# Moments ahead of a set-up chain, and PSUM banks handed out in adjacent pairs

## The chip, the cores and the metric

One core of one Trainium2 chip. The metric is the device time of one execution in microseconds (us), the median of the runs. The profile comes from one execution under the hardware profiler.

## The reference

Two layers, A and B, are applied in turn, twice, each on the layer norm of x and added to x (x is 2048 x 512, fp32).

```python
def _A_ref(x, w_r, w_i):
    X = rfft2(x); X = X * (w_r + 1j * w_i)
    return irfft2(X, s=(S, D))

def _B_ref(u, ...):
    K = einsum("dn,dnl,dn->dl", Cc, exp(dt*A*l), dt*Bc).real      # 512 x 2048 kernel of a state space
    y = irfft(rfft(u padded) * rfft(K padded))[:L]                # causal convolution, column by column
    return y + u * Dskip

x = x + _A_ref(_layernorm(x), ...)
x = x + _B_ref(_layernorm(x), ...)
x = x + _A_ref(_layernorm(x), ...)
x = x + _B_ref(_layernorm(x), ...)
```

## The kernel before

x lies in SBUF as 16 rows of [128, 512]. The Fourier transforms are matmuls with tables. The program is cut into pieces, Python generators that yield what their next step needs: an engine, a free tile of a ring, PSUM banks ("p:" and a kind), or an event such as `self.after(("in", 0))`. A planner, class Clock, holds a rough cost for each instruction and walks all pieces of a phase: among the steps that could start first by its own clock it emits the one with the smallest rank, the number given beside the piece. The order in which it emits is the order in each engine's queue; the hardware runs every queue in that order.

The first phase holds layer A of round 0 and the building of B's kernel K:

- `loads` sends the 8 pairs of x's rows on SP's queue, and between them the tables and, by `load_n`, the arrays kN (`ld` and two parts of `an`) from which K is made.
- `moments` (L494, L495) takes mean and variance of a row on DVE. `spread` (L502, L504, L507) makes the factors of four rows' norm, with a square root on ACT.
- `forward_a` normalises a row on ACT (L517), adds and subtracts its halves on POOL (L544 to L549), multiplies on PE (L562 to L571) and copies to SBUF on ACT (L576). `first_a` then needs all 16 rows: it folds (L589), multiplies by the weights (L687 to L704) and goes back (L713 to L725).
- The set-up, `setup_b` (rank -130; L1071 to L1117) and `setup_a` (-110; L1034 to L1049), is a chain of small DVE and ACT steps on kN. `setup_f` and `parts` split its results into three bf16 parts each by casts on ACT (L1020) and subtractions on DVE (L1026), which go to DRAM (`spe`, `spt`). When all 15 are there, `load_k` (L1126, L1127) brings back slices of them, and `exp_k` (L1135, L1151) and `unit_k` (L1165 to L1195) make K in 32 units.

Then ranks from -4 on mix the units with `first_a` and the inverse `inv_a`. In the second phase come B of round 0, A of round 1 (`forward_a` with r = 1, `group_a`, `inv_a`) and B of round 1. `group_b` makes a spectrum by matmuls into two banks X (L829), multiplies it by the kernel's on DVE (L929), combines on POOL (L935), and goes back on PE (L946) and ACT (L955); `group_a` does the like for A: L626, then L631 to L633 on DVE, L637 on POOL, L646 and L649 on PE. `forward_b` turns rows of x (L796, L798), `inv_b` adds B's result to x (L973, L979).

PSUM has 8 banks of 512 columns, shared out by kind:

```python
BANKS1, SAME1 = {'a': (0, 2, 4), 's': (6, 7)}, {'t': 's', 'h': 's', 'l': 's', 'x': 's', 'k': 'a'}
BANKS2 = {'x': (0, 1, 2, 3), 't': (4, 5), 'h': (6, 7)}
```

In the second phase a piece that wants two banks for its products asks for "p:x p:x" and gets any two of the four.

Of the kernel before, what the change touches and what calls it, by code (L numbers as in the profile page):

```python
# [11 lines left out]
OP = mybir.AluOpType  # L12
# [7 lines left out]
BANKS1, SAME1 = {'a': (0, 2, 4), 's': (6, 7)}, {'t': 's', 'h': 's', 'l': 's', 'x': 's', 'k': 'a'}  # L20
BANKS2 = {'x': (0, 1, 2, 3), 't': (4, 5), 'h': (6, 7)}

# [383 lines left out]
class Net:  # L406
# [28 lines left out]
    def psum(self, kind):  # L435
        kind = self.same.get(kind, kind)

        banks = self.banks[kind]

        def make(i):  # L440
            o = 512 * banks[i]
            return self.ps[:, o:o + (1024 if kind == "a" else 512)]
        return self.timer.tile("p:" + kind, make, len(banks))
# [26 lines left out]
    def loads(self):  # L470

        src = self.io["A_x"].rearrange("b (p s) d -> p (b s) d", p=128)
        for q in range(8):
            self.nc.sync.dma_start(self.x[:, 2 * q:2 * q + 2, :], src[:, 2 * q:2 * q + 2, :])
            self.mark("in", q)
            yield self.emitted(("in", q))
            for i, f in ((0, "load_ra"), (1, "load_n"), (5, "load_da"), (6, "load_h"), (7, "load_rb")):
                if i == q:
                    getattr(self, f)()
            if q == 1:  # L480
                self.mark("kN")
                yield self.emitted("kN")
# [51 lines left out]
    def forward_a(self, r, s2, st):  # L534
# [16 lines left out]
        if r:  # L551
# [5 lines left out]
            self.drop(uv)  # L557
        yield "PE p:x"
        p = self.psum("x")
        R, R2, nR = self.Ra[:, 1], self.Ra.rearrange("p a m -> p (a m)"), self.Ra[:, 2]  # L560
# [31 lines left out]
    def group_a(self, g):  # L592
# [29 lines left out]
        self.drop(AB)  # L622
        yield "PE p:x p:x"
        X = [self.psum("x")[:, :257] for sg in range(2)]
        for sg in range(2):
            nc.tensor.matmul(X[sg], ca[:, sg, :], V[:, sg, :257], start=True, stop=True)  # L626
        self.drop(V)
        yield "DVE t1a t2a"
        t1, t2 = (self.w(k, [128, 2, 258]) for k in ("t1a", "t2a"))
        for sg in range(2):  # L630
            nc.vector.tensor_tensor(t1[:, sg, :257], X[sg], W[:, 0, sg], op=OP.mult)  # L631
            nc.vector.scalar_tensor_tensor(t2[re, sg, :257], X[sg][im], -1.0, W[im, 1, sg], op0=OP.mult, op1=OP.mult)
            nc.vector.tensor_tensor(t2[im, sg, :257], X[sg][re], W[re, 1, sg], op=OP.mult)  # L633
        self.drop(*X)
        yield "POOL Za"
# [27 lines left out]
    def first_a(self, r, g):  # L663
# [16 lines left out]
        if r:  # L680
            nc.gpsimd.memset(Y2[:, 64:65], 0.0)
        yield "PE p:x p:x" if r else "PE p:a"
        X = [self.psum("x") for _ in range(2)] if r else [self.psum("a")]
        Xr, Xi = X if r else (X[0][:, :512], X[0][:, 512:])
        P, Q, nP = ca[:, 0, :], ca[:, 1, :], ca[:, 2, :]
# [12 lines left out]
        nc.vector.tensor_tensor(t2[:, 1, :], Xi[:, :257], W[:, 0, :257], op=OP.mult)  # L698
        self.drop(*X)
        yield "POOL Za"  # L700
# [99 lines left out]
    def forward_b(self, r, b, e, st):  # L800


        free = self.emitted(("group", 1), 16) if r else self.emitted(("inverse", 0), 16) if e else self.after("product", 32)
        yield "DVE a", self.after((id(st), b // 2) if not r else (id(st), b // 2, b % 2)), free
        xn = self.w("a", [128, 2, 256])
        for s in range(2):
            self.norm(2 * b + s, st, slice(256 * e, 256 * e + 256), xn[:, s])
        one = not (r or e)
        yield "PE p:a yd" if one else "PE p:x p:x iy"
        y = self.w("yd" if one else "iy", [128, 2, 512])  # L810
        self.turn_b([xn[:, 0], xn[:, 1]], y, "a" if one else "xx")
# [75 lines left out]
    def group_b(self, r, q, e):  # L887
# [16 lines left out]
        if new:  # L904
            y = self.w("yk", [128, 2, 2, 256])
            nc.sync.dma_start(y.rearrange("p g h d -> p g (h d)"), self.yk[1, two].rearrange("g c a b h d -> (c a b) g (h d)"))
            yield "PE p:x p:x", self.emitted("gk", q + 1)
            gk = self.gk[q]
            K = [self.psum("x") for _ in range(2)]
            self.spectrum(gk, [y[:, j] for j in range(2)], K)  # L910
            self.drop(gk, y)
            yield "ACT"
            for j in range(2):
                nc.scalar.copy(kh[:, j].rearrange("p r d -> p (r d)"), K[j])
            nc.scalar.dma_start(self.khat[:, two, :, d], kh)
            self.drop(*K)
            yield "+"
        Y = self.place[e][:, two].rearrange("p g (h d) -> p g h d", h=2)
        yield "PE p:x p:x", self.after(("rows", r, e), 8), self.after(("gi", r, q)), self.emitted(("added", r), 16)
        gi = self.gi[r, q]  # L920
        X = [self.psum("x") for _ in range(2)]
        self.spectrum(gi, [Y[:, j] for j in range(2)], X)
        names = ("t1b", "t2b", "Zb") if r else ("t1", "t2", "Z")
        yield f"DVE {names[0]} {names[1]}"
        t = [self.w(k, [128, 2, 2, 256]) for k in names[:2]]
        for j in range(2):
            for c in range(2):
                x = X[j].rearrange("p (r d) -> p r d", r=2)[:, c, None, :].to_broadcast([128, 2, 256])
                nc.vector.tensor_tensor(t[c][:, j], x, kh[:, j, ::-1, :] if c else kh[:, j], op=OP.mult)  # L929
        self.drop(*X, kh)  # L930

# [26 lines left out]
    def inv_b(self, r, b, e, st=None):  # L958
# [8 lines left out]
        late = not e and b > 4  # L967
        yield "PE p:x p:x" if late else "PE p:h p:t", self.emitted(("turned", r), 8 * late)
        q = [self.psum(k)[:, :256] for k in ("xx" if late else "ht")]
        for i in range(4):  # L970
# [5 lines left out]
        for s in range(2):  # L976
            s2 = 2 * b + s
            xs = self.x[:, s2, d]
            nc.vector.tensor_tensor(xs, xs, q[s], op=OP.add)  # L979
            self.drop(q[s])  # L980
            if st is None:
# [264 lines left out]
    def turn_k(self, q, i):  # L1246
# [6 lines left out]
        if i == 0:  # L1253
# [3 lines left out]
            if not last:  # L1257
                self.drop(sk)
        yield "PE p:x p:x" if last else "PE p:k", self.after(came)
        if last:  # L1260
            p = [self.psum("x") for _ in range(2)]
        else:
            p = self.psum("k")
            p = p[:, :512], p[:, 512:]
        for h in range(2):
            nc.tensor.matmul(p[h], self.Rk[:, h, :], KT, start=True, stop=True)
        if not last and i % 2:
            self.drop(self.kt[q, i // 2])
        for h in range(2):
# [15 lines left out]
            if last:  # L1285
                self.drop(p[h])
                yield "ACT"
# [92 lines left out]
    def plan_a(self, sb):  # L1380
# [126 lines left out]
```

## Time and profile before

| | |
|---|---|
| median of 3 runs | 789.07 us (786.17 to 793.95) |
| the profiled execution | 790.61 us, its span 788.8 us |
| PE busy | 651.1 us, 83% of the span |
| DVE busy | 508.4 us, 64% |
| ACT busy | 419.9 us, 53% |
| POOL busy | 304.1 us, 39% |
| mean granted clock of TensorE | 0.938 |

Busy time of PE includes that matmuls overlap in its pipeline, so 83% is not 83% of its peak. The first 80 us or so are set-up and the first forward transform; from there to about 346 us the 32 units of K run beside the rest of layer A; the second phase fills what remains. A number such as L562 is a line of the kernel file; the profile's groups name it with the engine, the operation and the tiles that are written and read.

### The profile page before, as it was taken

How to read it: one execution, taken by the hardware profiler on the slowest of the kernel's cores; microseconds unless marked ns; L12 is line 12 of the kernel's file. 1: busy time of each engine (PE TensorE's matmuls, PEld its weight loads, DVE VectorE, ACT ScalarE, POOL GpSimd, SP SyncE). 2: the span in 40 equal slices, each digit the busy share in tenths (PEclk: the TensorE clock that was granted, in tenths of full speed). 3: DMA queues.
4: the chain of work that ended last, by engine and by line, in shares of the span. 5: the costliest groups of instructions: out<-in, count | busy, mean ns of one | idle time of the engine just before them, and what ended most of it. 6: DMA issues, size and time to landing. Idle time of an engine off the chain costs nothing. (4 is left out here: it accounts for less than half of the span.)

```text
span 788.8 us, 23367 instructions
## 1 busy us (share of the span) xinstructions
PE 651.1 (83%) x9892; PEld 420.5 (53%) x9892; DVE 508.4 (64%) x1022; ACT 419.9 (53%) x768; POOL 304.1 (39%) x339
## 2 busy tenths in 40 slices
PE   4389888976988898998798679888877898697895
PEld 3277555544555443447444435767766554444565
DVE  5966569748758584884545435885767698376522
ACT  5766878887877967835244123375542334333120
POOL 4290346336335321420325223284433653076320
PEclk9699888997989998999999969999997999999999
DMA  9218302640623874738999933911655333966848
GB/s 329 62 25 295 108 17 78 206 123 14 208 77 120 302 242 141 224 124 191 255 260 262 300 128 97 317 78 47 219 204 194 121 73 92 211 197 160 241 107 269
DMA packets 76696, 132.50 MB, mean 168 GB/s; under 512 B 4684, under 2 KB 53584, under 8 KB 75952
## 3 DMA queue, kind: packets, MB, share of 16 engines
q1 hardware_dynamic: 42288, 93.26, 38.2%
q10 hardware_dynamic: 34304, 37.75, 17.1%
q8 instruction: 78, 1.28, 0.7%
q14 instruction: 26, 0.21, 0.1%
HBM read 70.31 MB, written 27.13 MB: 124 GB/s over the span
## 5 line engine op out<-in xcount | busy, mean ns | idle before, releaser
L1182 POOL TENSOR_TENSOR Y<-wk,Y 128x1024 f32<-128x1024 f32 x32 | 64.8, 2025 | 121.3 <-issue 73.4
L935 POOL TENSOR_TENSOR wk<-wk 128x512 f32<-128x512 f32 x32 | 40.0, 1274 | 102.0 <-DVE wk L929 83.9
L973 PE MATMUL ps<-wk,cRbT 64*128 64x256 f32 x512 | 64.5, 397 | 6.1 <-DMA wk<-Ya 3.7
L796 PE MATMUL ps<-wk,cRb 128*32 128x256 f32 x1024 | 60.1, 381 | 6.4 <-DVE wk L519 3.0
L798 ACT COPY wk<-ps 128x512 f32<-128x512 f32 x64 | 37.0, 586 | 51.5 <-PE ps L796 37.4
L929 DVE TENSOR_TENSOR wk<-ps,Y 128x512 f32<-128x512 f32 x64 | 39.5, 684 | 37.3 <-PE ps L829 29.0
L1135 PE MATMUL ps<-wk,Y 96*128 96x512 bf16 x128 | 44.7, 431 | 22.7 <-DVE Y L1178 10.3
L973 PEld LDWEIGHTS ps<-wk,cRbT 64*128 64x128 f32 x512 | 54.3, 195 | 16.7 <-issue 7.3
L562 PE MATMUL ps<-cRa,wk 128*128 128x256 f32 x128 | 36.7, 413 | 28.6 <-POOL wk L544 25.3
L1167 DVE SCALAR_TENSOR_TENSOR wk<-wk,ps 128x1024 f32<-128x1024 f32 x32 | 38.9, 1215 | 31.3 <-ACT wk L1165 31.2
L929 DVE TENSOR_TENSOR Y<-ps,wk 128x512 f32<-128x512 f32 x64 | 39.5, 684 | 24.7 <-issue 14.0
L796 PEld LDWEIGHTS ps<-wk,cRb 128*32 128x32 f32 x1024 | 38.4, 109 | 29.6 <-ACT wk L798 5.9
L979 DVE TENSOR_TENSOR x<-x,ps 128x256 f32<-128x256 f32 x64 | 24.8, 408 | 42.7 <-PE ps L973 42.5
L955 ACT COPY Ya<-ps 128x256 f32<-128x256 f32 x64 | 19.3, 386 | 60.0 <-PE ps L946 43.8
L1178 DVE TENSOR_TENSOR Y<-ps,Y 128x1024 f32<-128x1024 f32 x32 | 39.0, 1219 | 17.4 <-ACT ps L1171 17.4
L1151 ACT ACTIVATE Y<-ps 128x1024 f32<-128x1024 f32 x48 | 46.1, 1032 | 6.0 <-PE ps L1135 5.7
L1195 PEld LDWEIGHTS ps<-Y 128*32 128x32 f32 x2048 | 35.3, 123 | 24.1 <-issue 14.5
L745 PE MATMUL ps<-cDaT,apart 128*32 128x256 f32 (+1 forms) x256 | 46.4, 328 | 0.9 <-DVE wk L1206 0.8
L1195 PE MATMUL ps<-Y 128*32 128x64 f32 x2048 | 40.9, 240 | 6.2 <-ACT wk L678 2.5
L544 POOL TENSOR_TENSOR wk<-wk 128x256 f32<-128x256 f32 x32 | 25.9, 809 | 50.9 <-ACT wk L517 44.2
L935 POOL TENSOR_TENSOR wk<-Y 128x512 f32<-128x512 f32 x22 | 27.5, 1276 | 44.6 <-DVE Y L929 31.2
L946 PE MATMUL ps<-wk,Y 32*32 32x256 f32 x1344 | 38.4, 411 | 7.3 <-POOL wk L935 3.6
(218 smaller groups left out, 1648.2 us busy)
## 6 DMA issues: line engine op xcount, KB each, us to landing
Y<-in_GA_dram SPq DMA_DIRECT2D x12, 899.0 KB, 14.2
x<-in_PA_dram SPq DMA_DIRECT2D x16, 642.0 KB, 4.3
x<-in_A_x_dram SPq DMA_DIRECT2D x16, 512.0 KB, 6.7
yk<-wk ACTq DMA_DIRECT2D x32, 256.0 KB, 2.6
wk<-yk SPq DMA_DIRECT2D x16, 512.0 KB, 4.6
wk<-khat SPq DMA_DIRECT2D x16, 512.0 KB, 5.6
kd<-wk SPq DMA_DIRECT2D x4, 1024.0 KB, 3.9
khat<-wk ACTq DMA_DIRECT2D x8, 512.0 KB, 2.9
```

What stands on the lines that cost most here:

```text
L745: nc.tensor.matmul(p[32 * i:32 * i + 32, o:o + n], self.folded(r, i)[:, b, s2].rearrange("p g m -> p (g m)"), self.DaT[:, b, first:first + ...
L796: self.nc.tensor.matmul(p[o:o + 32, 256 * h:256 * h + 256], self.Rb[:, 2 * h + j, 32 * a:32 * a + 32], xn[s], start=True, stop=True)
L929: nc.vector.tensor_tensor(t[c][:, j], x, kh[:, j, ::-1, :] if c else kh[:, j], op=OP.mult)
L935: nc.gpsimd.tensor_tensor(Z[:, :, c], t[0][:, :, c], t[1][:, :, c], op=op)
L946: nc.tensor.matmul(v[j][h][i:i + 32], gi[o:o + 32, j, 4 + 2 * s + c, :], Z[o:o + 32, j, c, :], start=c == 0, stop=c == 1)
L973: nc.tensor.matmul(q[s], self.RbT[o, i, :], y[o, i, :], start=i == 0, stop=i == 3)
L1135: self.nc.tensor.matmul(p, f[:, c:c + 128], self.oh[:k, o:o + 512], start=True, stop=True)
L1151: nc.scalar.activation(m[:, :, 1024:] if i == 2 else m[:, i, :1024], p.rearrange("p (i m) -> p i m", i=2) if i == 2 else p, AF.Exp)
L1167: nc.vector.scalar_tensor_tensor(s, c, MAGIC, p, op0=OP.subtract, op1=OP.subtract)
L1178: nc.vector.tensor_tensor(E[:, 1, :1024], p, m[:, :1024], op=OP.mult)
L1182: nc.gpsimd.tensor_tensor(E[:, 0, :1024], c, m[:, :1024], op=OP.mult)
L1195: nc.tensor.matmul(pk[32 * j:32 * j + 32, 64 * e:64 * e + 64], E1[:, r, i, :], E2[:, r, i], start=r == 0, stop=r == 1)
```

## The change

Two things are edited.

In the first phase, kN is loaded after x's fourth pair of rows in place of its second, and the moments and the spreads of x get rank -131 in place of -120, so that they go ahead of `setup_b` (-130) wherever the planner finds both ready.

In the second phase, banks 0 to 3 are handed out as two pairs of adjacent banks, kind "w", 1024 columns each. `group_a` and `group_b` read a pair with one DVE instruction where two read one bank each; a copy of the kernel's spectrum reads a pair with one ACT instruction. `forward_a` of the second round takes a whole pair for its 512 columns, as do the late `inv_b`, `forward_b`, `first_a` and the last quarter of `turn_k`, and a pair comes free as a whole. `turn_k` also gets a mark, by which its second half of a slice is emitted only after its first. The diff, cut:

```diff
-BANKS2 = {'x': (0, 1, 2, 3), 't': (4, 5), 'h': (6, 7)}
+BANKS2 = {'w': (0, 2), 't': (4, 5), 'h': (6, 7)}
@@ psum
-            return self.ps[:, o:o + (1024 if kind == "a" else 512)]
+            return self.ps[:, o:o + (1024 if kind in "aw" else 512)]
@@ loads
-            for i, f in ((0, "load_ra"), (1, "load_n"), (5, "load_da"), (6, "load_h"), (7, "load_rb")):
+            for i, f in ((0, "load_ra"), (3, "load_n"), (5, "load_da"), (6, "load_h"), (7, "load_rb")):
...
-            if q == 1:
+            if q == 3:
                 self.mark("kN")
@@ forward_a
-        yield "PE p:x"
-        p = self.psum("x")
+        yield "PE p:w" if r else "PE p:x"
+        p = self.psum("w" if r else "x")[:, :512]
@@ group_a
-        yield "PE p:x p:x"
-        X = [self.psum("x")[:, :257] for sg in range(2)]
+        yield "PE p:w"
+        X = self.psum("w").rearrange("p (s f) -> p s f", s=2)[:, :, :257]
         for sg in range(2):
-            nc.tensor.matmul(X[sg], ca[:, sg, :], V[:, sg, :257], start=True, stop=True)
+            nc.tensor.matmul(X[:, sg], ca[:, sg, :], V[:, sg, :257], start=True, stop=True)
...
-        for sg in range(2):
-            nc.vector.tensor_tensor(t1[:, sg, :257], X[sg], W[:, 0, sg], op=OP.mult)
-            nc.vector.scalar_tensor_tensor(t2[re, sg, :257], X[sg][im], -1.0, W[im, 1, sg], op0=OP.mult, op1=OP.mult)
-            nc.vector.tensor_tensor(t2[im, sg, :257], X[sg][re], W[re, 1, sg], op=OP.mult)
-        self.drop(*X)
+        nc.vector.tensor_tensor(t1[:, :, :257], X, W[:, 0], op=OP.mult)
+        nc.vector.scalar_tensor_tensor(t2[re, :, :257], X[im], -1.0, W[im, 1], op0=OP.mult, op1=OP.mult)
+        nc.vector.tensor_tensor(t2[im, :, :257], X[re], W[re, 1], op=OP.mult)
+        self.drop(X)
@@ first_a
-        yield "PE p:x p:x" if r else "PE p:a"
+        yield "PE p:w" if r else "PE p:a"
@@ forward_b
-        yield "PE p:a yd" if one else "PE p:x p:x iy"
+        yield "PE p:a yd" if one else "PE p:w iy"
@@ group_b
-            yield "PE p:x p:x", self.emitted("gk", q + 1)
+            yield "PE p:w", self.emitted("gk", q + 1)
...
-            for j in range(2):
-                nc.scalar.copy(kh[:, j].rearrange("p r d -> p (r d)"), K[j])
+            nc.scalar.copy(kh.rearrange("p j r d -> p (j r d)"), K)
...
-        X = [self.psum("x") for _ in range(2)]
-        self.spectrum(gi, [Y[:, j] for j in range(2)], X)
+        X = self.psum("w")
+        self.spectrum(gi, [Y[:, j] for j in range(2)], (X[:, :512], X[:, 512:]))
...
-        for j in range(2):
-            for c in range(2):
-                x = X[j].rearrange("p (r d) -> p r d", r=2)[:, c, None, :].to_broadcast([128, 2, 256])
-                nc.vector.tensor_tensor(t[c][:, j], x, kh[:, j, ::-1, :] if c else kh[:, j], op=OP.mult)
-        self.drop(*X, kh)
+        for c in range(2):
+            x = X.rearrange("p (j r d) -> p j r d", j=2, r=2)[:, :, c, None, :].to_broadcast([128, 2, 2, 256])
+            nc.vector.tensor_tensor(t[c], x, kh[:, :, ::-1, :] if c else kh, op=OP.mult)
+        self.drop(X, kh)
@@ inv_b
-        yield "PE p:x p:x" if late else "PE p:h p:t", self.emitted(("turned", r), 8 * late)
-        q = [self.psum(k)[:, :256] for k in ("xx" if late else "ht")]
+        yield "PE p:w" if late else "PE p:h p:t", self.emitted(("turned", r), 8 * late)
+        if late:
+            w = self.psum("w")
+            q = w[:, :256], w[:, 512:768]
+        else:
+            q = [self.psum(k)[:, :256] for k in "ht"]
@@ turn_k
-        yield "PE p:x p:x" if last else "PE p:k", self.after(came)
+        yield "PE p:w" if last else "PE p:k", self.after(came), self.emitted(("turning", q, i // 2), 0 if last else i % 2)
...
+        self.mark("turning", q, i // 2)
@@ plan_a
         for s2 in range(16):
-            yield -120, moments(s2)
+            yield -131, moments(s2)
             if s2 % 4 == 3:
-                yield -120, self.spread(s2 // 4, st, NORMS[0])
+                yield -131, self.spread(s2 // 4, st, NORMS[0])
```

More of the change, by code (lines that the diff above doesn't have):

```diff
@@ L681, in first_a @@
             nc.gpsimd.memset(Y2[:, 64:65], 0.0)
-        yield "PE p:x p:x" if r else "PE p:a"
-        X = [self.psum("x") for _ in range(2)] if r else [self.psum("a")]
-        Xr, Xi = X if r else (X[0][:, :512], X[0][:, 512:])
+        yield "PE p:w" if r else "PE p:a"
+        X = self.psum("w" if r else "a")
+        Xr, Xi = X[:, :512], X[:, 512:]
         P, Q, nP = ca[:, 0, :], ca[:, 1, :], ca[:, 2, :]
@@ L698, in first_a @@
         nc.vector.tensor_tensor(t2[:, 1, :], Xi[:, :257], W[:, 0, :257], op=OP.mult)
-        self.drop(*X)
+        self.drop(X)
         yield "POOL Za"
@@ L808, in forward_b @@
         one = not (r or e)
-        yield "PE p:a yd" if one else "PE p:x p:x iy"
+        yield "PE p:a yd" if one else "PE p:w iy"
         y = self.w("yd" if one else "iy", [128, 2, 512])
-        self.turn_b([xn[:, 0], xn[:, 1]], y, "a" if one else "xx")
+        self.turn_b([xn[:, 0], xn[:, 1]], y, "a" if one else "w")
         self.drop(xn)
@@ L906, in group_b @@
             nc.sync.dma_start(y.rearrange("p g h d -> p g (h d)"), self.yk[1, two].rearrange("g c a b h d -> (c a b) g (h d)"))
-            yield "PE p:x p:x", self.emitted("gk", q + 1)
+            yield "PE p:w", self.emitted("gk", q + 1)
             gk = self.gk[q]
-            K = [self.psum("x") for _ in range(2)]
-            self.spectrum(gk, [y[:, j] for j in range(2)], K)
+            K = self.psum("w")
+            self.spectrum(gk, [y[:, j] for j in range(2)], (K[:, :512], K[:, 512:]))
             self.drop(gk, y)
             yield "ACT"
-            for j in range(2):
-                nc.scalar.copy(kh[:, j].rearrange("p r d -> p (r d)"), K[j])
+            nc.scalar.copy(kh.rearrange("p j r d -> p (j r d)"), K)
             nc.scalar.dma_start(self.khat[:, two, :, d], kh)
-            self.drop(*K)
+            self.drop(K)
             yield "+"
         Y = self.place[e][:, two].rearrange("p g (h d) -> p g h d", h=2)
-        yield "PE p:x p:x", self.after(("rows", r, e), 8), self.after(("gi", r, q)), self.emitted(("added", r), 16)
+        yield "PE p:w", self.after(("rows", r, e), 8), self.after(("gi", r, q)), self.emitted(("added", r), 16)
         gi = self.gi[r, q]
-        X = [self.psum("x") for _ in range(2)]
-        self.spectrum(gi, [Y[:, j] for j in range(2)], X)
+        X = self.psum("w")
+        self.spectrum(gi, [Y[:, j] for j in range(2)], (X[:, :512], X[:, 512:]))
         names = ("t1b", "t2b", "Zb") if r else ("t1", "t2", "Z")
@@ L979, in inv_b @@
             nc.vector.tensor_tensor(xs, xs, q[s], op=OP.add)
-            self.drop(q[s])
+            if s or not late:
+                self.drop(w if late else q[s])
             if st is None:
@@ L1258, in turn_k @@
                 self.drop(sk)
-        yield "PE p:x p:x" if last else "PE p:k", self.after(came)
[L1260 to L1264, printed above, removed]
+        yield "PE p:w" if last else "PE p:k", self.after(came), self.emitted(("turning", q, i // 2), 0 if last else i % 2)
+        w = self.psum("w" if last else "k")
+        p = w[:, :512], w[:, 512:]
         for h in range(2):
             nc.tensor.matmul(p[h], self.Rk[:, h, :], KT, start=True, stop=True)
+        self.mark("turning", q, i // 2)
         if not last and i % 2:
@@ L1285, in turn_k @@
             if last:
-                self.drop(p[h])
+                if h:
+                    self.drop(w)
                 yield "ACT"
```

## The prediction

> **What bounds the kernel now.** I read first the page and the busy time by stretches of 20 us, to see where the engines stand still; then the waits and the timeline of the first 85 us, where the change moves work; then the groups and waits of the stretches where the second phase uses the banks that the diff renames. Columns of the stretches: us, busy of PE, weight loads, DVE, ACT, POOL, granted clock, DMA share, GB/s.
>
> ```profile
> span 788.8 us, 23367 instructions
> ...
> 0.00:20.00 20.00, 8.75 (x42) 7.83 (x43) 10.97 (x25) 10.73 (x15) 9.19 (x16) 1.00 0.91 326
> 20.00:40.00 20.00, 6.59 (x29) 5.74 (x29) 19.09 (x37) 14.48 (x18) 5.31 (x10) 0.66 0.22 59
> 40.00:60.00 20.00, 16.76 (x109) 15.11 (x108) 13.45 (x20) 13.47 (x24) 17.84 (x27) 1.00 0.15 41
> 60.00:80.00 20.00, 18.75 (x139) 15.48 (x138) 11.75 (x22) 11.44 (x25) 1.91 (x3) 1.00 0.83 293
> ...
> 77.80:300.00 222.20, 189.46 (x2722) 115.69 (x2721) 152.95 (x242) 180.88 (x216) 95.16 (x69) 0.91 0.42 136
> ```
>
> From 77.8 to 300 us ACT is busy 180.88 of 222.2 us and PE 189.46: a dense stage that little can shorten, but that can begin sooner. Before it lies a thin one: from 20 to 40 us PE works 6.59 us of 20 while DVE works 19.09. The waits of the first 85 us say what PE misses, the timeline why (start, duration, engine, line).
>
> ```profile
> POOL wk L544 <- ACT wk L517: 25.3, 3, 14.1
> PE ps L562 <- POOL wk L544: 24.6, 2, 13.4
> ...
> 11.38 1.27 DVE L1071 TENSOR_TENSOR Y<-Y 128x1024 f32<-128x1024 f32 x1 [1.88 <-DMA Y<-in_kN_dram]
> ...
> 28.49 0.30 ACT L502 ACTIVATE rs<-mv,eps 128x4 f32<-128x4 f32 x1
> ...
> 33.49 0.75 POOL L544 TENSOR_TENSOR wk<-wk 128x256 f32<-128x256 f32 x1 [14.08 <-ACT wk L517]
> ...
> 50.25 0.84 DVE L1049 SCALAR_TENSOR_TENSOR Y<-Y 128x512 f32<-128x512 f32 x1
> ...
> 54.48 0.81 ACT L517 ACTIVATE wk<-x,nb,rs 128x512 f32<-128x512 f32 x1 [0.71 <-POOL wk L549]
> ...
> 55.20 1.12 ACT L1020 CAST Y<-Y 128x512 bf16<-128x512 f32 x2
> ...
> 55.84 0.69 DVE L1026 TENSOR_TENSOR Y<-Y 128x512 f32<-128x512 f32 x1 [4.75 <-ACT Y L1020]
> ...
> 58.57 0.83 DVE L1117 TENSOR_TENSOR Y<-Y 128x512 f32<-128x512 f32 x1
> ...
> 63.70 2.05 PE L589 MATMUL ps<-cDa,Ya 128*128 128x128 f32 x16 [1.25 <-ACT Ya L576]
> ...
> 67.33 0.62 ACT L1020 CAST Y<-Y 128x512 bf16<-128x512 f32 x1 [0.21 <-DVE Y L1026]
> ...
> 73.83 0.92 SPq L1126 DMA_DIRECT2D Y<-spe  x1
> ...
> 79.83 1.94 ACT L1151 ACTIVATE Y<-ps 128x1024 f32<-128x1024 f32 x2 [0.79 <-PE ps L1135]
> ```
>
> Read it as two chains on the same DVE. Set-up begins at 11.38, when kN has landed, and takes nearly all of DVE; the moments of x's rows stand in its gaps. So the second spread's root (L502) comes only at 28.49, POOL and PE stand still for 14.08 and 13.4 us, and the forward rows 4 to 15 fall into 33.5 to 63 us. There they fill ACT's queue: the first cast of the set-up (L1020) waits behind the last norm (L517, 54.48) until 55.20, and DVE, whose next instruction needs that cast, stands still for 4.75 us although L1049 was done by 51.1. L1117 ends the set-up at 59.40, the last cast ends at 67.95, the factors are loaded at 73.83, and the first exponential of the products runs at 79.83. The dense stage starts there. So the end of the set-up's chain and the place of the forward rows set this stage.
>
> **The first part of the change**, moments at rank -131 and load_n after x's fourth pair. It removes and adds no instruction.
>
> ```profile
> L494 DVE BATCH_NORM_STATS2 st<-x 128x6 f32<-128x512 f32 x16 | 10.7, 672 | 4.4 <-DMA x<-in_A_x_dram 4.4
> L1020 ACT CAST Y<-Y 128x512 bf16<-128x512 f32 x15 | 8.5, 621 | 0.2 <-DVE Y L1026 0.2
> L1026 DVE TENSOR_TENSOR Y<-Y 128x512 f32<-128x512 f32 x10 | 6.5, 687 | 6.9 <-ACT Y L1020 6.7
> ...
> L495 DVE BATCH_NORM_AGGREGATE mv<-st 128x2 f32<-128x6 f32 x16 | 2.9, 182 | 0.6
> ...
> 14.09 1.10 DVE L1075 TENSOR_TENSOR Y<-Y 128x512 f32<-128x512 f32 x1
> ...
> 21.60 0.68 DVE L1086 TENSOR_TENSOR Y<-Y 128x512 f32<-128x512 f32 x1
> ```
>
> Queue: kN's three DMAs (ld and two of an) go behind two more pairs of x on SP, 2 x 512 KB = 1.05 MB at the 326 GB/s of the first 20 us, so kN lands 3.2 us later, at 14.6. The x pairs behind it land when they did. DVE: a row's moments cost 0.67 + 0.18 = 0.85 us. Rows 4 to 7 (3.4 us) now run while DVE waits for kN, where it idled 1.88 us before; rows 8 to 15 stay ahead of the set-up's remaining instructions as their pairs land.
>
> When is L1117 done? Before, 11.38 to 59.40 is 48.0 us. Put at 14.6 this gives 62.6. Off go rows 4 to 7 with their spread (3.4 + 0.35), the stall of 4.75, for ACT's queue is then free of norms, and the one L1026 (0.6) that stood ahead: 53.5. On comes the sharing with POOL: a 128x512 two-input instruction takes 1.10 us with POOL's forward work beside it (L1075) and 0.68 without (L1086). Of the set-up some 6 us ran while POOL stood still; at 1.10/0.68 that adds 3.7 at most, and I take 3. So L1117 ends at 56.5, 2.9 us earlier. The bounds: 53 if sharing costs nothing, 60 if also the moments' absence leaves gaps of 3.5 us where ACT computes logarithm and root.
>
> Then the tail. It took 8.5 us from L1117 to the last cast, with forward copies and fold copies between. All 15 casts are 8.5 us of ACT and 10 subtractions 6.5 us of DVE; with four of the five arrays ready before L1117, some 5.5 us are left behind it. Last cast at 62 instead of 67.95: **6 us**, bounds 2 and 10. The DMAs behind it (spe, spt, loads) move with it. The forward rows cost POOL about 2.0 us each (17.84 us for 27 instructions, three a row, from 40 to 60) and run without the pause of 13.4 us, so the 16th, from 10 us on and with some waits between, ends near 45 to 48 and the folds (63.70) begin by then; this only puts more filler ahead of the products. I pass the 6 us on to the end, since the stage behind is dense and everything in it depends on these factors.
>
> The Trainium skill, "SBUF — State Buffer", Who interferes with whom, says that a VectorE instruction with two SBUF inputs and a GpSimd instruction that reads SBUF exclude each other for whole instructions. The trace shows 1.10 against 0.68, a part of that. By the rule some three more forward rows than before under the set-up, at 2.0 us of POOL, would cost 6 in place of my 3, and the sum would be -5.
>
> **Second part: pairs of banks.** In group_a six DVE instructions a group become three of twice the columns.
>
> ```profile
> L696 DVE TENSOR_TENSOR x<-ps,x 128x514 f32<-128x514 f32 x16 | 11.1, 691 | 1.7 <-PE ps L688 0.5 <-DVE x L704 0.4 <-DMA spt<-Y 0.2
> ...
> L632 DVE SCALAR_TENSOR_TENSOR Ya<-ps,Y 64x257 f32<-64x257 f32 x24 | 10.3, 428 | 0.7
> L631 DVE TENSOR_TENSOR Ya<-ps,Y 128x257 f32<-128x257 f32 x24 | 10.2, 423 | 0.5
> L633 DVE TENSOR_TENSOR Ya<-ps,Y 64x257 f32<-64x257 f32 x24 | 10.1, 420 | 0.7
> ...
> L646 PE MATMUL ps<-Y,Ya 128*64 128x128 f32 x176 | 15.0, 324 | 10.4 <-POOL Ya L606 7.0 <-POOL Ya L637 3.4
> ```
>
> Before 2 x (0.423 + 0.428 + 0.420) = 2.54 us, after 3 x 0.691 = 2.07: 0.47 a group, 7 us over 15. Here it can count, as PE stands still 10.4 us before L646, whose weights POOL adds from what DVE multiplies. The first product waits for both banks, which costs half a matmul pair where DVE has no backlog. I take 3 of the 7; bounds 0 and 7.
>
> In group_b four instructions become two.
>
> ```profile
> L1178 DVE TENSOR_TENSOR Y<-ps,Y 128x1024 f32<-128x1024 f32 x32 | 39.0, 1219 | 17.4 <-ACT ps L1171 17.4
> ...
> 410.15 4.88 DVE L929 TENSOR_TENSOR wk<-ps,Y 128x512 f32<-128x512 f32 x8 [0.49 <-PE ps L829]
> ```
>
> Back to back eight of them take 4.88, so 0.61 each and 2.44 a group; two of 1.219 are 2.44 as they stand, and about 2.3 overlapped alike. So 0 to 0.15 us a group: I take 0.5 us for 32, bounds -1 (two halves released later) and 5. The joined kh copies, turn_b, turn_k, the late inv_b and first_a keep as many tiles in flight as before: nothing, bounds 1 either way.
>
> Where the change takes something away is forward_a of the second round: a whole pair for 512 columns, two tiles in flight instead of four.
>
> ```profile
> 515.60 1.03 PE L562 MATMUL ps<-cRa,wk 128*128 128x256 f32 x4
> ...
> 517.35 1.05 ACT L576 COPY Y<-ps 128x512 f32<-128x512 f32 x2
> 517.42 0.68 PE L566 MATMUL ps<-cRa,wk 128*128 128x128 f32 x4 [0.79 <-DVE wk L554]
> ...
> 525.64 1.03 PE L562 MATMUL ps<-cRa,wk 128*128 128x256 f32 x4
> ...
> 527.12 1.03 PE L562 MATMUL ps<-cRa,wk 128*128 128x256 f32 x4
> 527.32 0.58 ACT L576 COPY Y<-ps 128x512 f32<-128x512 f32 x1
> ```
>
> In the steady part a tile takes 1.48 us of PE (525.64 to 527.12) and its copy is 0.58 right behind: two suffice. In the ragged part the tile of 515.60 would wait for a copy that ends near 517.9, behind which PE's later matmuls queue. About 2 us at one or two places, less the 0.79 that PE waited anyway: **+1.5**, bounds 0 and 5.
>
> **Sum**: -6 - 3 - 0.5 + 1.5 = -8. The profiled execution took 790.61 us, 1.5 above the median 789.07; 790.6 - 8 - 1.5 gives 781.
>
> **Rivals.**
> (1) Slower: the set-up comes late. kN is 3.2 us late for certain, the instructions that ran beside an idle POOL (6 us) may nearly double, as the 128x512 two-input rows do by 1.6, and without moments to fill DVE's waits for ACT 5 us more open. Then L1117 ends at 53.5 + 6 + 5 = 64.5, 5 us late, with the tail kept at 8.5; with forward_a's 1.5 and nothing gained in the second phase, 789.1 + 5 + 1.5 = 795.5. It decides where the load of the factors passes 73.83. For it: DVE is 19.09 of 20 busy. Against: the sum of DVE's work is unchanged, and 4.75 us of pure stall hang on ACT's queue. 0.18.
> (2) More: the freed 13.4 us of PE count too, since a fold and products of two more groups are done ahead and lighten the dense stage, and group_a gives its 7 us: 774. For it PE's 189 of 222; against, ACT would have to keep up. 0.17.
> (3) Absorbed: the dense stage ends on something with its own pace, as the DMAs of the layer behind; 2 us are left: 787. 0.12.
> (4) Two pairs are too few: each of 16 forward tiles and the group's products wait out a copy of 0.58, 9 us; with the first part's 6 gained and nothing else, 792. The steady cadence of 1.48 speaks against it. 0.08. The Trainium skill, "Perfetto Trace Analysis", Optimizing Tensor Performance, wants independent groups of matmuls to rotate through different banks so that one's eviction overlaps the next; it speaks for this rival, as half of each pair then stands empty.
>
> **How the numbers follow.** The forecast, 776 to 786, has 0.45. A measurement of this kernel tells about 1% (8 us) from no change. The forecast's middle lies on that line, so it gives half to each side: faster 0.22 + 0.17, about 0.38; same 0.23 + 0.12 + 0.02, 0.37; slower 0.18 + 0.06 and a rest, 0.25. The range 770 to 797 leaves out the ends of (1) and (2).
>
> **What would show it.** Right: the root of the second spread (L502) near 13 us; no pause of over 5 us of POOL or PE before 45; the first fold before 52; the factors' load near 68 and the first exponential near 74; in group_a three products of 0.69 a group; in forward_a's second round PE waits for L576 of 2 us in all. Wrong: the load at 73.83 or later; or an early load and a late end of the products; or PE waiting for bank pairs throughout 500 to 540.

## The result, and the profile after

The changed kernel takes 782.54 us (median of 20 runs, 778.68 to 790.55), the kernel before 792.42 (20 runs). The ratio is 0.9893, interval 0.9869 to 0.9918, or about 8.5 us less; the two medians lie 9.9 us apart. The forecast of -8 us and 781 came out, but partly by luck. Of its parts one was missing and one was much too small, and they cancelled; and it started from 789.07, the median of three runs, where twenty runs give 792.42.

The profile after comes from a long execution (span 787.6, so about 789), so single stages in it read some us late. First the stretches of 20 us, columns as before.

```profile
0.00:20.00 20.00, 6.60 (x28) 5.92 (x29) 12.54 (x35) 8.76 (x14) 7.20 (x15) 1.00 0.90 322
20.00:40.00 20.00, 18.48 (x117) 16.13 (x115) 10.71 (x20) 15.38 (x25) 18.28 (x29) 1.00 0.68 205
40.00:60.00 20.00, 16.48 (x95) 14.76 (x96) 16.91 (x24) 14.53 (x24) 6.13 (x10) 0.91 0.12 45
60.00:80.00 20.00, 14.81 (x89) 11.49 (x90) 12.95 (x25) 11.58 (x23) 1.92 (x3) 0.83 0.44 141
```

From 20 to 40 us PE now works 18.48 us where it had 6.59: forward rows moved there. DVE fell from 19.09 to 10.71 in the same stretch: the set-up's chain now waits there for something other than DVE. The waits of the first 85 us and the timeline say for what.

```profile
POOL wk L544 <- ACT wk L517: 14.3, 4, 12.2
PE ps L562 <- POOL wk L544: 13.9, 2, 13.4
DVE rs L504 <- ACT rs L502: 6.1, 3, 4.4
DVE Y L1092 <- ACT Y L1090: 5.2, 1, 5.2
```

```profile
14.54 1.40 DVE L1073 TENSOR_TENSOR Y<-Y 128x1024 f32<-128x1024 f32 x1 [0.35 <-DMA Y<-in_kN_dram]
...
26.52 0.18 DVE L504 RECIPROCAL rs<-rs 128x4 f32<-128x4 f32 x1 [4.39 <-ACT rs L502]
...
28.04 1.06 ACT L1080 ACTIVATE Y<-Y 128x1024 f32<-128x1024 f32 x1
...
40.87 1.04 ACT L1090 ACTIVATE Y<-Y 128x1024 f32<-128x1024 f32 x1
...
41.94 0.93 DVE L1092 TENSOR_TENSOR Y<-Y 128x512 f32<-128x512 f32 x1 [5.18 <-ACT Y L1090]
...
52.88 2.05 PE L589 MATMUL ps<-cDa,Ya 128*128 128x128 f32 x16 [0.67 <-ACT Ya L576]
...
60.16 0.69 DVE L1119 TENSOR_TENSOR Y<-Y 128x512 f32<-128x512 f32 x1
...
67.03 1.22 ACT L1022 CAST Y<-Y 128x512 bf16<-128x512 f32 x2 [0.20 <-DVE Y L1028]
...
70.13 0.92 SPq L1128 DMA_DIRECT2D Y<-spe  x1
...
77.80 1.02 ACT L1153 ACTIVATE Y<-ps 128x1024 f32<-128x1024 f32 x1 [0.62 <-PE ps L1137]
```

PE's pause in the middle (13.41 us ahead of 34.30 before) is gone; the 13.4 us that the waits still list stand before its first row. The folds begin at 52.88 for 63.70. kN is there at 14.54, as worked out. But the set-up hardly got shorter, 46.31 us for 48.02: its Square (L1090 after, L1088 before) runs at 40.87 where it ran at 21.72, since ACT's queue now has norms of the forward rows ahead of it, and DVE stands still 4.39 us for the root of the third spread (L502) and 5.18 us for the Square. L1119 ends at 60.85, 1.45 us later than L1117 did before. The last cast ends at 68.25, for 67.95 before. And yet the load of the factors is at 70.13 for 73.83, and the first exponential at 77.80 for 79.83.

What moved the load is SP's queue. The weights of `first_a` come in loads of 642 KB each (in_PA_dram). Before, five of them stood between the stores of the casts' results (spe, spt); now these five stand ahead of the stores, from 18 us on. The queue's rows, its wait and the median time from issue to landing, before and then after, with the first row of PE behind its new pause:

```profile
56.77 2.63 SPq L670 DMA_DIRECT2D x<-in_PA_dram  x5
...
67.80 3.59 SPq L1021 DMA_DIRECT2D spe<-Y  x6
...
SPq L1021 <- DMA x<-in_PA_dram: 5.2, 4, 1.5
spe<-Y SPq DMA_DIRECT2D x12, 128.0 KB, 5.4
```

```profile
18.07 20.20 SPq L669 DMA_DIRECT2D x<-in_PA_dram  x5
...
spe<-Y SPq DMA_DIRECT2D x12, 128.0 KB, 1.7
...
68.31 1.20 PE L686 MATMUL ps<-wk,x 128*128 128x257 f32 x2 [5.18 <-ACT Y L1022]
```

A store took 5.4 us to land and now takes 1.7, and the load follows the last cast by 1.88 us where it followed by 5.88. Part of this is lost again: PE now stands still 5.18 us up to 68.31, behind an ACT queue that is full of casts, and from 65 to 70 us the granted clock is 0.56, where it was 1.00 before. Of the 3.7 us at the load 2.0 are left at the first exponential.

In the second phase (group_a's products are L630 to L632 after, their weights' users L645):

```profile
L645 PE MATMUL ps<-Y,Ya 128*64 128x128 f32 x192 | 14.0, 291 | 9.3 <-POOL Ya L636 5.0 <-POOL Ya L606 4.1
...
L631 DVE SCALAR_TENSOR_TENSOR Ya<-ps,Y 64x514 f32<-64x514 f32 x12 | 8.4, 697 | 0.4
L632 DVE TENSOR_TENSOR Ya<-ps,Y 64x514 f32<-64x514 f32 x12 | 8.3, 689 | 0.4
L630 DVE TENSOR_TENSOR Ya<-ps,Y 128x514 f32<-128x514 f32 x12 | 8.3, 688 | 0.5 <-PE ps L626 0.4
```

```profile
L926 DVE TENSOR_TENSOR wk<-ps,Y 128x1024 f32<-128x1024 f32 x32 | 37.5, 1217 | 42.7 <-PE ps L828 17.4 <-issue 10.2 <-ACT Y L952 8.4
```

```profile
522.70 1.78 PE L562 MATMUL ps<-cRa,wk 128*128 128x256 f32 x4 [2.29 <-ACT Y L576]
```

A group of group_a costs DVE 0.688 + 0.697 + 0.689 = 2.07 us, as forecast; group_b's two products are 2 x 1.217; forward_a's second round waits once, 2.29 us, for a pair to come free.

The stretch from round 1's first fold (L589) to the first matmul of `forward_b` behind it (L796, L795 after) holds group_a. Here it is before and after, columns as in the other stretches:

```profile
536.80:632.60 95.80, 78.80 (x814) 62.34 (x818) 65.95 (x176) 38.48 (x138) 43.51 (x72) 0.93 0.48 162
```

```profile
541.90:629.80 87.90, 75.09 (x818) 60.29 (x822) 56.94 (x131) 38.38 (x138) 43.58 (x72) 0.96 0.52 176
```

It is 7.9 us shorter, and DVE is busy 9.0 us less in it.

### The profile page after: what moved, and what is told of

Read it like the earlier page. It is cut to its first block, busy times and chain, and to the rows that moved or that the text cites. A ratio compares the mean times of both kernels' runs of the same rounds, so it can differ in the third digit from the quotient of the medians.

```text
span 787.6 us, 23224 instructions
## 1 busy us (share of the span) xinstructions
PE 651.6 (83%) x9892; PEld 420.1 (53%) x9892; DVE 495.9 (63%) x913; ACT 417.1 (53%) x759; POOL 303.4 (39%) x339
## 5 line engine op out<-in xcount | busy, mean ns | idle before, releaser
L974 PE MATMUL ps<-wk,cRbT 64*128 64x256 f32 x512 | 68.3, 413 | 6.7 <-issue 2.9
L974 PEld LDWEIGHTS ps<-wk,cRbT 64*128 64x128 f32 x512 | 56.9, 205 | 18.8 <-issue 9.0
L795 PE MATMUL ps<-wk,cRb 128*32 128x256 f32 x1024 | 61.1, 386 | 6.1 <-DVE wk L519 2.4
L926 DVE TENSOR_TENSOR wk<-ps,Y 128x1024 f32<-128x1024 f32 x32 | 37.5, 1217 | 42.7 <-PE ps L828 17.4
L1137 PE MATMUL ps<-wk,Y 96*128 96x512 bf16 x128 | 42.2, 405 | 17.1 <-DVE Y L1180 8.3
L926 DVE TENSOR_TENSOR Y<-ps,wk 128x1024 f32<-128x1024 f32 x32 | 37.4, 1218 | 26.4 <-issue 17.6
L795 PEld LDWEIGHTS ps<-wk,cRb 128*32 128x32 f32 x1024 | 34.3, 111 | 34.8 <-ACT wk L797 4.6
L1197 PEld LDWEIGHTS ps<-Y 128*32 128x32 f32 x2048 | 34.9, 122 | 27.1 <-issue 11.6
L1197 PE MATMUL ps<-Y 128*32 128x64 f32 x2048 | 40.4, 238 | 8.0 <-ACT wk L748 3.4
L1167 ACT ACTIVATE wk<-ps,magic 128x1024 f32<-128x1024 f32 x32 | 35.1, 1116 | 17.4 <-PE ps L1137 11.2
```

What stands on the lines that cost most here:

```text
L795: self.nc.tensor.matmul(p[o:o + 32, 256 * h:256 * h + 256], self.Rb[:, 2 * h + j, 32 * a:32 * a + 32], xn[s], start=True, stop=True)
L926: nc.vector.tensor_tensor(t[c], x, kh[:, :, ::-1, :] if c else kh, op=OP.mult)
L974: nc.tensor.matmul(q[s], self.RbT[o, i, :], y[o, i, :], start=i == 0, stop=i == 3)
L1137: self.nc.tensor.matmul(p, f[:, c:c + 128], self.oh[:k, o:o + 512], start=True, stop=True)
L1197: nc.tensor.matmul(pk[32 * j:32 * j + 32, 64 * e:64 * e + 64], E1[:, r, i, :], E2[:, r, i], start=r == 0, stop=r == 1)
```

## The experiments

Ratios are to the kernel before, run on the same chip in turn; each of the three rounds has a chip of its own, and each kernel 6 or 12 runs. "Products end" gives the start of the last matmul of K's products (L1195 before, L1197 after) in the one profile of a kernel; before it is 346.2.

**First round: the parts alone.** The first part alone, three edits on the kernel before:

```diff
-            for i, f in ((0, "load_ra"), (1, "load_n"), ...
+            for i, f in ((0, "load_ra"), (3, "load_n"), ...
-            if q == 1:
+            if q == 3:
-            yield -120, moments(s2)
+            yield -131, moments(s2)          # the spread below it likewise
```

> Before with the first part alone (kN behind x's fourth pair, moments and spreads at rank -131). Theory 1, the prediction's: the first part gives 6 of the 8 us, so the ratio to before is about 0.992 (0.988 to 0.997) and the dense stage's end is some 6 us earlier. Theory 2, from the changed kernel's profile, where the first exponential came only 2.0 us earlier (77.80 for 79.83) and the last matmul of the products 4.8 us later (351.0 for 346.2): the first part gives nothing, 1.000 (0.997 to 1.004).

Ratio 0.996 (0.9931 to 0.9988), which lies in theory 1's range, at half of its size. In this kernel, which has no mark in `turn_k`, a slice's tile can be loaded anew before its first half is turned, so a part of K is computed from another slice; its instructions and sizes are the same, and it stands here for its time alone. The kernel before has no mark either, but in its order this does not happen.

The second part alone is the changed kernel with those edits undone:

> Before with the second part alone (banks in pairs). Theory 1: 2 us, ratio 0.997 (0.993 to 1.001). Theory 2: all of the gain, 0.990 (0.986 to 0.993), most of it in group_a, whose stretch from the first to the last fold took 65.1 us before and 59.3 in the changed kernel's profile.

0.9966 (0.9936 to 0.9995), theory 1's size.

> The changed kernel as it is, for a second profile and on the same chip as the others: 0.989 (0.986 to 0.992). If its products end again near 351, the first part loses time in the dense stage; if near 340 to 346, the first profile was of a long execution (787.6 us of span where the median is 782.5).

0.9872 (0.9823 to 0.9921). Products end at 347.3 in this profile and at 351.0 in the first: between the two cases, and in both later than before.

```diff
-        nc.vector.tensor_tensor(t1[:, :, :257], X, W[:, 0], op=OP.mult)
+        for sg in range(2):
+            nc.vector.tensor_tensor(t1[:, sg, :257], X[:, sg], W[:, 0, sg], op=OP.mult)
+            ...                              # the two products into t2 likewise
```

> The changed kernel with group_a's three products split again into six, one bank each; the banks stay pairs. Both theories: DVE has 0.47 us more a group. Theory 1: 3 us of the gain go, ratio 0.993. Theory 2: 6 to 7 us go, 0.997 to 0.998. If pairing acts through the banks and not through the instructions, it stays at 0.989.

0.9965 (0.9932 to 0.9998): against the changed kernel's 0.9893 and 0.9872, group_a's shorter products alone are worth 0.7 to 0.9%, 6 to 7 us. The stretch that holds group_a is long again:

```profile
536.20:630.80 94.60, 77.17 (x816) 61.02 (x820) 65.88 (x176) 38.52 (x138) 43.58 (x72) 0.95 0.49 164
```

It takes 95.8 to 96.6 us in the four profiles with single banks, 94.6 here, and 86.5 to 90.1 in the nine with pairs and merged products. The granted clock, 0.95 here for 0.96 in the changed kernel, does not make the difference. Neither theory had it all: the first part gives something (against theory 2), group_a gives twice the 3 us of theory 1, and the second part alone gives less than group_a's products in it. Something in the second part's kernel had to cost time. Its profile showed the place: its products end at 355.7, before at 346.2, though this kernel's first phase differs from the kernel before only by turn_k's mark.

**Second round: the mark.**

```diff
-        yield "PE p:x p:x" if last else "PE p:k", self.after(came)
+        yield "PE p:x p:x" if last else "PE p:k", self.after(came), self.emitted(("turning", q, i // 2), 0 if last else i % 2)
...
+        self.mark("turning", q, i // 2)
```

> Before with turn_k's mark alone (the second half of a slice is emitted only after its first). In before's order, slices 0 and 1 were turned with the second half ahead of the first. Theory 3, from the profiles so far: the prediction costed the mark at nothing, but it is the third part of the change and costs the first phase 7 to 9 us (products end at 355.7 in the second part's kernel, which has it, for 346.2 before); the ratio is 1.008 to 1.012. Theory 1, the mark is nothing: 1.000 (0.997 to 1.003), products' end 346.

1.011 (1.0059 to 1.0161); products end at 356.6. Theory 3 holds, theory 1 falls: the line that the prediction passed over costs 1.1%, 8.7 us (5 to 13 by the interval). The PE rows that turn K's first quarter, two slices of two halves each, in the kernel before, then in this one, and the DVE step L1256 in both:

```profile
150.30 1.99 PE L1266 MATMUL ps<-wk,cRk 128*128 128x512 f32 x4
...
153.89 1.99 PE L1266 MATMUL ps<-wk,cRk 128*128 128x512 f32 x4
...
156.84 2.10 PE L1266 MATMUL ps<-wk,cRk 128*128 128x512 f32 x4
...
170.52 1.89 PE L1266 MATMUL ps<-wk,cRk 128*128 128x512 f32 x4
```

```profile
158.84 3.78 PE L1266 MATMUL ps<-wk,cRk 128*128 128x512 f32 x4 [4.88 <-DVE Y L1178]
164.41 1.99 PE L1266 MATMUL ps<-wk,cRk 128*128 128x512 f32 x4
173.31 1.89 PE L1266 MATMUL ps<-wk,cRk 128*128 128x512 f32 x4
175.66 1.99 PE L1266 MATMUL ps<-wk,cRk 128*128 128x512 f32 x4
```

```profile
152.48 1.13 DVE L1256 TENSOR_TENSOR wk<-wk 1x128 f32<-1x128 f32 x1
```

```profile
150.36 1.12 DVE L1256 TENSOR_TENSOR wk<-wk 1x128 f32<-1x128 f32 x1
```

The first half of a quarter's first slice has a small DVE step in front of it (L1256), which stands in DVE's queue behind products. Without the mark the planner turned a second half first: three of four turns fell into 150 to 159, between products. With it nothing may be turned until the first half's matmul is emitted, and that matmul is placed behind products; PE, in order, stands still 4.88 us there until L1178 lets go of its banks. Two turns come as late as 173 to 178, with their copies and DMA issues between ACT's work for the next units. The kernel copy (L1206) of unit 12 is at 192.35 for 187.12, the last at 357.06 for 346.90.

> Before with the first part and the mark. Theory 3: the first part gives 6 to 8 us in the first phase and the mark takes 7 to 9, so the products end at 347 as in the changed kernel and the ratio is about 1.000. Theory 1: 0.996, as the first part without the mark.

1.0019 (0.9987 to 1.0051): theory 3's ratio, though the products end at 351.8 and not at 347. On top of the mark the first part gives 0.9%.

```diff
-        yield "PE p:w" if last else "PE p:k", self.after(came), self.emitted(("turning", q, i // 2), 0 if last else i % 2)
+        yield "PE p:w" if last else "PE p:k", self.after(came)
...
-        if not last and i % 2:
+        if not last and self.halves[q, i // 2] == 2:
             self.drop(self.kt[q, i // 2])
```

> The changed kernel without the mark: the halves of a slice may be turned in either order, and the slice's tile is dropped when both are done. Theory 3 with the order as its cause: the mark's 7 us come back, the products end at 340 to 342 and the ratio to before is 0.980 to 0.983. Theory 3 with the tile's longer life as its cause: as the changed kernel, 0.988. Theory 1: 0.988.

0.9797 (0.975 to 0.9844), median 778.15: the order was the cause, not the tile's longer life, which this kernel keeps. Freed by count, a tile still cannot be loaded anew before both of its halves are turned, so the mark's protection stays without its order. This kernel beats both others. The gain came back, if not all of it at the place expected: the products end at 343.8 in its profile.

```diff
-        for c in range(2):
-            x = X.rearrange("p (j r d) -> p j r d", j=2, r=2)[:, :, c, None, :].to_broadcast([128, 2, 2, 256])
+        for j in range(2):
+            for c in range(2):
+                x = X.rearrange("p (j r d) -> p j r d", j=2, r=2)[:, j, c, None, :].to_broadcast([128, 2, 256])
...
```

> The changed kernel with group_b's two products split again into four, one bank each; the banks stay pairs. The prediction has 0.5 us for this in the sum: the ratio to before stays at 0.988 to 0.989. If reading a pair in one instruction is worth what the means say (4 x 0.684 against 2 x 1.219 us, 0.3 us for 32 groups), it goes up by 0.006 at most, with half of it more likely since DVE waits in that stage.

0.9877 (0.9823 to 0.9931): group_b's merged products are worth nothing that shows, as forecast. The interval, half a per cent to either side, does not rule out the 0.003 that the expectation called the likelier.

**Third round: how the parts add up, and which half of the first part acts.**

The kernel without the mark, that is the second part with the tile freed by count, without both edits of the first part:

```diff
-            for i, f in ((0, "load_ra"), (3, "load_n"), ...
+            for i, f in ((0, "load_ra"), (1, "load_n"), ...
...
-            if q == 3:
+            if q == 1:
-            yield -131, moments(s2)
+            yield -120, moments(s2)          # the spread below it likewise
```

> The second part alone, without the mark; a slice's tile is dropped when both halves are turned. With the mark the second part went from 1.011 to 0.997, 1.4%, where the prediction had 2 us. Theory 4: that is its size, 7 us of it group_a's shorter products and the rest the pairs; without the mark the ratio is 0.985 to 0.989. Theory 1: the prediction's 2 us, 0.997; then most of the 1.4% was a recovery of what the mark takes.

0.9951 (0.9911 to 0.9991): between the two theories; its interval still holds the prediction's 0.997, though the plain medians of the same runs, 785.28 and 792.15, give 0.991. Eight kernels now stand in one table:

| ratio to before | neither part | first part | second part | both |
|---|---|---|---|---|
| without the mark | 1 | 0.996 | 0.995 | 0.980 |
| with the mark | 1.011 | 1.002 | 0.997 | 0.989 |

Over its four pairs the first part gives 0.4 to 1.5%, mean 0.9% (7 us); the second 0.5 to 1.6%, mean 1.2% (10 us); the mark takes 0.2 to 1.1%, mean 0.7% (6 us). Each cell is uncertain by some 0.3 to 0.5% and each kernel has its own plan, so the spread within a row is not read further.

The next two undo one of these edits each, again on the kernel without the mark. The load back, the rank kept:

```diff
-            for i, f in ((0, "load_ra"), (3, "load_n"), ...
+            for i, f in ((0, "load_ra"), (1, "load_n"), ...
...
-            if q == 3:
+            if q == 1:
```

> The changed kernel without the mark and with load_n back after x's second pair; the moments' rank stays at -131. kN lands near 11.4 in place of 14.6, but the moments of rows 4 to 15 now stand ahead of the set-up only from there on. If the rank alone makes the first part's gain, the ratio is 0.978 to 0.980 and the first exponential comes at 75 or earlier; if the load's place is part of it, 0.983 to 0.988.

0.982 (0.9774 to 0.9866), median 776.81; the first exponential's factors are on PE at 74.1, the exponential at 74.72.

The rank back, the later load kept:

```diff
-            yield -131, moments(s2)
+            yield -120, moments(s2)          # the spread below it likewise
```

> The changed kernel without the mark and with the rank back at -120; load_n stays after x's fourth pair. Rows 4 to 7 take their moments while DVE waits for kN, rows 8 to 15 stand in the set-up's gaps again. If the load's place makes the gain: 0.980. If the rank does: 0.986 to 0.990, about the second part alone, as kN is 3.2 us later and the later forward rows wait as before.

0.9893 (0.9844 to 0.9942), products' first factors at 78.0. The rank makes the gain and the place of the load does not show: with the rank the median is 777 to 778 wherever kN is loaded. The intervals of this run and the one before touch between 0.9844 and 0.9866. Which of the two fast kernels, with the load early or late, is better stays open.

```diff
+        self.mark("square")                  # behind the set-up's Square
...
-        yield ("DVE a" if r else "ACT a"), self.after((id(st), s2 // 4)), self.emitted(("grouped", 0, 1), 8 * r)
+        yield ..., *(() if r or s2 < 8 else (self.emitted("square"),))
```

> The changed kernel without the mark, and forward rows 8 to 15 are emitted only after the set-up's Square. In the changed kernel DVE stood still 4.39 and 5.18 us while the set-up's root and Square stood behind norms in ACT's queue, and L1119 ended at 60.85, 1.4 us later than L1117 before, where 2.9 us earlier was forecast. If that queue is the cause, L1119 ends 4 to 8 us earlier, the first exponential comes at 68 to 72 for 77, and the ratio is 0.971 to 0.976. If the forward rows, now later, hold up folds and products instead, it stays at 0.980 or goes above.

0.9916 (0.9882 to 0.995), where the kernel without the hold has 0.9797: about 1% slower. The first statement of the expectation failed, the second came true. The rows of its profile:

```profile
33.24 1.06 ACT L1090 ACTIVATE Y<-Y 128x1024 f32<-128x1024 f32 x1 [1.58 <-DVE Y L1086]
...
54.50 1.14 ACT L1022 CAST Y<-Y 128x512 bf16<-128x512 f32 x2
...
69.55 0.62 ACT L1022 CAST Y<-Y 128x512 bf16<-128x512 f32 x1 [1.02 <-DVE Y L1028]
...
80.42 4.70 ACT L1154 ACTIVATE Y<-ps 128x1024 f32<-128x1024 f32 x5
```

```profile
57.38 1.10 DVE L1120 TENSOR_TENSOR Y<-Y 128x512 f32<-128x512 f32 x1
...
62.85 1.90 DVE L1028 TENSOR_TENSOR Y<-Y 128x512 f32<-128x512 f32 x3 [2.65 <-ACT Y L1022]
```

Against the kernel without the hold (free_drop's profile) the Square comes 6.9 us earlier (33.24 for 40.15), but the set-up ends only 0.9 us earlier, at 58.48 for 59.37. DVE's stalls in the set-up fell from 11.2 to 8.0 us, while its instructions took 28.5 us for 26.3: with POOL's forward rows now beside them, rows such as L1015 take 1.10 us where they took 0.69. The held-back rows meet the casts in ACT's queue, as they did before the change, and the weights of `first_a` are back between the stores, at 56.08. So the last cast ends at 70.17 for 66.17, the load is at 74.21 for 68.04, and the products start at 80.42 for 75.88.

The thirteen profiles without the hold, put together by the rank of the moments, show what the first part moved. The medians, in us from the start:

| | set-up ends | last cast ends | load of the factors | first exponential |
|---|---|---|---|---|
| rank -120 (5 profiles) | 59.1 | 67.6 | 73.6 | 79.5 |
| rank -131 (8 profiles) | 59.5 | 66.3 | 68.2 | 76.1 |
| forecast | 56.5 | 62 | near 68 | near 74 |

With rank -120 the load follows the last cast by 5.5 to 6.5 us, with rank -131 by 1.9 us in every profile. So at the load the first part bought little by a shorter set-up (none) or by earlier casts (1.3 us) and 4 us by the stores, whose way the weights had left. That the weights' place makes these 4 us is read from the queue's waits; no run moves the weights alone.

## Why the prediction was right or wrong

**The stage.** Right: PE's pause in the middle and the late forward rows were what could be saved. The pause is gone, the fold is 10.8 us earlier.

**Term "6 us" for the first part.** The size held (0.9% on the mean, 7 us, within the bounds 2 to 10), the path to it did not. The step "L1117 ends at 56.5" failed: it ended at 60.85 in this profile, outside the bounds 53 to 60, and at 59.5 on the median of eight, no earlier than without the rank (59.1). The moments came off as worked out: 11.5 us of DVE in the set-up before, 7.6 after. But DVE stood still 12.55 us of it where it had stood still 8.90 and where 4.75 fewer were forecast. Of the stalls I had listed the absence of moments in the gaps (3.5 us at most), but not that ACT's queue, relieved of norms at the casts, gets them at the third spread's root and at the set-up's Square: 4.39 + 5.18 us. That was the very queue I had just called free. Nor did the 3 us for sharing with POOL come: the set-up's own instructions took 26.2 us for 27.6.

The tail was mis-sized too. From the set-up's end to the last cast's end (68.25) it took 7.4 us, where 5.5 was forecast and 8.5 was measured before; so the last cast came 0.3 us late here, 1.3 early on the medians, and not 6. That the load is near 68 on the median all the same is luck. The DMAs behind the casts did not just "move with it": the stores lost the weights from between them, which no term had, and that brought 4 us. From the load to the first exponential some 2 us are lost again, at PE's new pause, so the exponential moved 2.0 us in one profile, 3.6 in the other (76.27) and 3.4 on the medians, not 6. The rest of the 7 us must come from filler done ahead, rival (2) in part; that last sentence is argued from the earlier folds, not shown by a run of its own.

Of the signs, the root of the second spread came (13.34), the fold nearly (52.88), the first exponential did not (77.80 for 74). One sign of being wrong came as well, an early load and a late end of the products: they end at 351.0 and 347.3 for 346.2, and the mark makes that end late.

**Term "3 us" for group_a.** The instruction prices were right (2.54 to 2.07 a group), the share of the 7 us that reaches the end was not: splitting them again took 6 to 7 us. I had read the row of L646 as 10.4 us of PE waiting for what POOL adds from DVE's products; only 3.4 of them are on that addition (L637), the other 7.0 on L606, where POOL fills a tile with zeros. The row that bears the reading is POOL's own wait: from 537 to 632 us L637 waits 21.4 us for DVE's last product (L633). I halved the term for the later first product, whose price never showed.

**Terms 0.5 for group_b and +1.5 for forward_a.** The first held within what split_b can tell. For the second, the stretch from the last product of B's first layer to the first fold of round 1 took 53.0 to 54.0 us in the four profiles with single banks (median 53.6) and 53.5 to 56.2 in the ten with pairs (median 54.05); a wait of 2.29 us stands in the longest of these. That is about 0.5 us, within the bounds 0 to 5, and it was not isolated.

**What was costed at nothing.** "turn_k ... keep as many tiles in flight as before: nothing" looked at the banks and passed over the mark in the same function: 8.7 us alone, about 6 on the mean. The price could have been seen: the quarter's first half waits for L1256, which the trace of before has at 152.48, after the first turn at 150.30, so halves were turned out of order there and a rule against it had to move something. Nor is the line idle: with the first part and without the mark (a_only) a slice's tile can be loaded anew too early. The cheaper guard is the free by count.

So the sum was -6 - 3 - 0.5 + 1.5 = -8 and the pieces on the mean -7 (first part), -10 (second, 6 to 8 of it group_a), +6 (mark). They add up to -11, where the changed kernel measured -8.5 and -10 (0.9893 and 0.9872); the difference is within the uncertainty of the cells. What the second part's other 2 to 4 us are is not settled: B's second layer, from its first to its last product, took 60.5 to 63.8 us with single banks and 57.5 to 63.4 with pairs, which overlap.

**The rivals.** (1) was wrong in its end and right in a step: the set-up was late, its tail was not. (2) came true in part, with group_a's 7 us. (3) does not show: 3.4 us at the first exponential are 2.5 us at the products' end without the mark and 8.5 with it, on the medians. (4) is out. The rule of the Trainium skill, "Perfetto Trace Analysis", Optimizing Tensor Performance, that independent groups of matmuls should rotate through different banks, speaks for it; two pairs were enough here but for one wait of 2.29 us. Of the rule of the Trainium skill, "SBUF — State Buffer", Who interferes with whom, the stage's sum decides little: neither the 6 us worked out from it nor the 3 us in its place came. Single rows fit it: L1075 before took 0.42 us more beside POOL than L1086 took alone, about as much as POOL's L548 takes alone (0.45 at 17.02); the prediction called this a part of the rule's price.

## What to carry to other kernels

Read every line of a diff for what it orders, also the one that looks like bookkeeping: here one condition on the order of emission cost about as much as the first part gave. Freeing a queue at one place fills it at another, so name for each engine, and for the DMA queue, what stands in line before and after a move: here the stores' queue gave 4 us that nobody had planned. Where the next engine waits for one engine's instructions, as POOL did for DVE's products in group_a, a saving on these can count in full.

## What was not expected of the hardware

Merging two reads into one that spans two adjacent banks saves a little each time, but the mean durations do not say how much. By them it is 2 x 0.423 against 0.688 us, 0.16, for 257 columns, and 2 x 0.684 against 1.217, 0.15, for 512. Recorded durations of neighbours overlap, though, so what counts is the time from start to start. Eight products of group_b took 4.88 us before (at 410.15), and the same work in four takes

```profile
419.90 4.62 DVE L926 TENSOR_TENSOR wk<-ps,Y 128x1024 f32<-128x1024 f32 x4 [3.81 <-issue]
```

That is 0.065 us a merge. In group_a six products took 2.72 us from start to start (563.18 to 565.90) and three take 2.16 (567.01 to 569.17), 0.19 a merge. It is worth 6 to 7 us in group_a, and nothing that shows in group_b.
